# A fused attention, expert and feed-forward kernel: the first pair's q and k loaded in three pieces of columns in place of two

## The chip, the cores and the metric

The kernel runs on one core of a Trainium2 chip. The metric is the device time of one execution in microseconds (us): 481.08 us before the change, the median of three runs (480.73 to 481.11).

## The reference, cut to what matters

Three layers follow each other on a batch of 4 sequences of 448 rows. The first is causal attention with 12 heads of 64; the second routes rows to the best two of 4 experts, each an attention of its own; the third is a feed-forward block with a short convolution and a gate. Only the first touches the change:

```
batch, n_heads, seq, head_dim = (4, 12, 448, 64)
scores = scale * np.matmul(q, k.transpose(0, 1, 3, 2))
mask = np.triu(np.ones((seq, seq), dtype=bool), k=1)
scores = np.where(mask, -1000000000.0, scores)
scores = scores - np.max(scores, axis=-1, keepdims=True)
attn = np.exp(scores)
attn = attn / (np.sum(attn, axis=-1, keepdims=True) + 1e-09)
return np.matmul(attn, v).astype(np.float32)
```

The second and third layers (`_moe_ref`, `_moe2_ref`) take the result as `x`; their code is left out here, since nothing of theirs is edited.

## The kernel before

**Tiling.** Heads are handled in pairs, one head on partitions 0 to 63 and the other on 64 to 127. A sequence of 448 is cut into NQ = 4 blocks of CP = 112 rows. The mask is causal, so block i of the queries meets only the first 112 x (i+1) keys: the score of block 0 needs columns 0 to 111 of q and k, that of block 1 columns 0 to 223, that of block 2 columns 0 to 335, that of block 3 all of them.

**The first pair.** For batch 0 the pairs are "plain": `load_plain` brings q and k of both heads as one transfer of 448 KB into the tile `sk_A`. The very first pair differs: `load_left` (L563) brings columns 0 to 223 and `load_right` (L566) columns 224 to 447, 224 KB each. `pair_scores` multiplies q by k (L630) block by block, from block 0 up for this pair alone, and both heads one after the other in each block. `j.ready` lists the load that a block waits for: the left half for blocks 0 and 1, the right half for 2 and 3. Each score then goes through the row maximum on VectorE (L686), the exponential on ScalarE (L695), the division by the row sum (L347 or L349), the transposition on TensorE (L726) and the product with v (L797).

**What sets the order.** Every piece of work is a task, added with an engine, an estimated cost, the tasks that it needs and a `lag` (for a load, the estimated time from issue to landing; LAND is 2600 ns). The order in which the tasks are issued on all engines is written out by hand in the table ORDER, as numbers of tasks. `Program.run` walks this table and issues the tasks; on each engine they then run in that order, held only by semaphores. While it walks, `run` also keeps an estimated clock for each engine. It is used for one thing: where the estimate says that TensorE will sit idle for over 700 ns before its next task, `run` calls `fill` (`warm`, L1587), which puts so many multiplications of the 128x128 identity in front of that task:

```
if start - end[e] > 700:
    fill(int((start - end[e] - 200) / (260 if end[e] > COLD else 430)), end[e])
```

These fill multiplications write to a bank that nothing reads and wait for nothing but the engine. A task that `need`s a load starts, by this estimate, no earlier than the load's end plus its lag; that holds for a load that needs a load as well.

**The queue of SyncE (SP).** All loads at the start are issued by SP, in order: the left half, then two pairs of expert weights (`praw`, L950 and L951), the right half, the convolution weights, and the second pair's q and k (L558).

Of the kernel before, what the change touches and what calls it, by code (L numbers as in the profile page):

```python
# [35 lines left out]
    "xry9H9wXnQ!RRci4JAe@k$R*J=|Lut9mou_3)O={fDmXr8bEd-zaWFC1nM*L0+~aNqXtm-NDxYnMxpSiUy09%@39}S&xwB^#t=K$m&75|3~C<r"
    "0rd&RMo%DS5O%B!8^T^8chSR`bMyiF4n2WcM6IF@P^YLHlmJaZYtR<78x5e7=!fVB=p*zg8i`rM%wrC)N7yam5s`{HM=?sT(5zB%sj_s3ctb>z"
    "Mlm?dBIXvAM}aUbj1VKocrnwM6XFJD2XjZ<$KXMim~QkSnhNSgvq3bJ0Tl*~p(oJ8Xbt8Y@dxG<+gjRQI#xPgDg;fG1~6t!0@H!%EA7K{VfKi}"
    "m_tk!Gk{^CKqMTgwWy=0yXX~Bh>C&kF(@nzi^C3-Qb|LlY*J_G9Pur2h1f?LBTbMDrM6OU=>iET&4LC<o1`VuEP5WjgqD#&SQhppT7;b@nMpFx"
    "5NVaPP1+~rNi>Rr!lo>iPM5BgZkB2(dXkvrAtgwCMIMR_tHow19i%SOBTy#@#zXT4i$;njiU3NkC_^Ih=sXXvj|cEBu)UxhZvZq58sPcJ0rD;B"  # L40
    "taPumjS?W4DPKxIm0pzIm$vfSc{z}P5~FlcdMQ_>Aj%a9MZr;Su=iL{5wa*ren1{0Z;|ul_ryOytDsBL83{rrkSSyiSwJQf@pxjMk~am?^X5Q9"
    "lw&f2+)sH)nIKP-H$gj~N90cOQ}Q@vfxJXsCGUfF$a&Bi=o$GEL@VMHiHa0Ox*|)Fy9mNp@MkH@l)phBFcORh5Ajwh<Gd}(HigD#^A|u=u$IpT"
    "i@{3p9{HTy$&2x3cmn=4`6n642bIk8R(Njycght-LDrHzC4D8WB|ym^_EkHMAK>4Bbl_acJZ00qV^5VHQ1<P4yM_FT_kp*{JK&x2@D5yw8Eodq"
    "`2!{GC9_2fMaxC&MK`<`<gKFJA~*Oa1yKT}DyXeg3>8PEJLuG}_ALJy|1n?e;8MTYukCksup?Y_$m=Yjm5i6%@`g%~j(m~V(N2w(%#_F-z0|!T"
    "R*9(OwCJMfJ?$0P&f_^!Me`+Ehuxtov6Qqs9y@M|?u$HBfXXQr6|a=YO7avf^@P&K|He}k_wYyfkm4L)S8Of5pk7n|qDiP>@Fd?;94}trZ_qx`"
    "X81ty5+7AeEr!sLw0`PpiJ3~H$!QxUG3s{7LCI-JkK;4#nd6q)ft$p2QV&aTv~2OiVm57<dR~&Fb{0P^?!w`VZ%UpOKQEpJ-<AN58Qf8E(!s$C"
    "@k_XQu!bg}1@Z0pC9s9|vUsX^ruc2~9Cd}dQv8Pc1~*PUrd`r{aF9|&shjqYwg!&lH^KPQwc;2!L(78O!5@lOaWUEp#wg>3;}^#d+7x4svCcm&"
    "4$wCE>(pJU48KP`q7LGQaXZDIi!X}1z`fvS;G1F{9zsXb?~5V0ZSZICDDH%6!SC=ls4jdr4T0;Sb>eAsHeEp9#61V^;4X1raG!Asx|<%LYw3fu"
    "G1>$TkE7w%=@;~CI+&5c579R12XqcDPw&MK;6*qEPKW!4W8Cp4<8RuGW8SgkSaTp4X8J81M?a>Y;cjrZI0&AAr{d@EQ}~zo=lG9~-x({6cZ~n$"
    "e_(tCTX8NNfJ@;J_-)4l1H!yu#Oc?J1^gm@n|{j}1Fz$E@%xS}y`P?EP?>nfF$2lOF~9Kt$-j2|bikZchM1vY9D!L(wDT8S-f`lPF@(%E`niM4"  # L50
# [1601 lines left out]
```

## Time and profile before

| | |
|---|---|
| median of 3 runs | 481.08 us (480.73 to 481.11) |
| time of the profiled execution | 481.08 us |
| its span, first to last instruction | 479.3 us |
| around the span | 1.78 us |
| TensorE (PE) busy | 470.7 us, 98% of the span |
| VectorE (DVE), ScalarE (ACT), GpSimd (POOL) busy | 391.0, 347.4, 332.5 us |
| DMA | 93.26 MB, 195 GB/s on average |

PE is matrix multiplication, PEld the loading of its weights. A busy PE is not a useful PE: the fill multiplications count as busy too. One multiplication in f32 leaves two MATMUL records in the trace, so six fill multiplications show as x12. The work before microsecond 30 is a short sequence of few instructions, and the timeline there can be read one by one.

### The profile page before, as it was taken

To read this page: it belongs to the slowest core of one execution; us is meant where nothing else is said; L and a number is where in the kernel's file an instruction comes from. 1 tells how busy PE (TensorE), PEld (TensorE's weight loads), DVE (VectorE), ACT (ScalarE), POOL (GpSimd) and SP (SyncE) were. 2 spreads that over 40 slices of the span, in tenths; PEclk is the share of its full clock that TensorE was granted. 3 is DMA by queue.
4 is the path that set the end of the run, shared out by engine and by line. 5 is a ranking of instruction groups with operands and counts; after the bars stand their busy time and mean duration, and the time that the engine had idled before them with its cause. 6 is when DMAs were issued, how large, how long until landed. Compare 5 with 4: busy or idle time off the path is not lost.

```text
span 479.3 us, 9963 instructions
## 1 busy us (share of the span) xinstructions
PE 470.7 (98%) x3114; PEld 398.2 (83%) x3114; DVE 391.0 (82%) x1154; ACT 347.4 (72%) x966; POOL 332.5 (69%) x475
## 2 busy tenths in 40 slices
...
GB/s 216 197 227 93 218 171 236 277 271 177 218 217 180 283 251 181 196 157 203 251 212 133 175 166 205 275 77 247 198 226 214 276 291 128 234 216 77 40 77 96
DMA packets 45845, 93.26 MB, mean 195 GB/s; under 512 B 4832, under 2 KB 27232, under 8 KB 45792
## 3 DMA queue, kind: packets, MB, share of 16 engines
...
q8 instruction: 24, 0.39, 0.4%
q10 hardware_dynamic: 432, 0.34, 0.2%
...
## 4 chain that ended last, share of the span: by engine, by line
PE 84%; DVE 5%; POOL 4%; ACT 3%; issue 1%; DMA 1%; SPq 0%; POOLq 0%; ACTq 0%; DVEq 0%
PE bank L1471 22%; PE bank L797 11%; PE bank L991 11%; PE bank L726 10%; PE bank L673 9%; PE bank L1338 8%; PE bank L1042 6%; PE bank L918 3%; PE bank L630 2%; DVE P_A L686 2%; ACT P_A L695 2%; PE bank L1587 1%; DMA sk_M<-sk_M 1%; POOL P_M L349 1%; POOL P_A L349 1%
## 5 line engine op out<-in xcount | busy, mean ns | idle before, releaser
L695 ACT ACTIVATE P_A<-P_A,nm_A 112x224 f32<-112x224 f32 (+3 forms) x192 | 99.9, 525 | 10.3 <-DVE nm_A L686 9.7
L686 DVE CUSTOM_DVE_ANT_0 P_A<-bank,mask 112x448 f32<-112x448 f32 (+3 forms) x192 | 79.7, 441 | 10.0 <-PE bank L630 6.1
L356 POOL TENSOR_TENSOR sk_A<-nat,sk_A 64x448 fp32r<-64x448 f32 (+1 forms) x67 | 77.5, 1158 | 5.4 <-ACT sk_A L347 1.5
L991 PE MATMUL bank<-xT,wqk 128*128 128x448 f32 x288 | 66.9, 372 | 0.0
L726 PE MATMUL bank<-ident,P_A 112*112 112x112 f32 x480 | 60.6, 262 | 2.6 <-ACT PT_A L347 1.9
L726 PEld LDWEIGHTS bank<-ident,P_A 112*112 112x112 f32 x480 | 48.3, 133 | 9.4 <-ACT PT_A L347 2.7
L349 POOL TENSOR_SCALAR P_A<-P_A,r_A 112x112 f32<-112x112 f32 (+3 forms) x95 | 48.1, 519 | 10.0 <-DVE r_A L706 8.2
L991 PEld LDWEIGHTS bank<-xT,wqk 128*128 128x128 f32 x288 | 51.7, 188 | 3.9 <-DVE nm_A L686 0.2
L673 PE MATMUL bank<-sk_A 128*112 128x224 f32 (+3 forms) x288 | 52.0, 306 | 0.2 <-DVE nm_A L686 0.2
L1359 DVE SCALAR_TENSOR_TENSOR bank<-h,cw,bank 128x448 f32<-128x448 f32 x64 | 42.6, 685 | 9.2 <-ACT bank L1357 7.7
L797 PE MATMUL bank<-PT_A,v 112*64 112x448 f32 (+3 forms) x384 | 49.9, 404 | 0.0
L347 ACT ACTIVATE P_A<-P_A,r_A 112x224 f32<-112x224 f32 (+3 forms) x94 | 46.7, 527 | 2.8 <-DVE r_A L706 1.6
L1471 PE MATMUL bank<-up,ws 128*128 128x448 f32 x198 | 46.7, 367 | 0.0
L347 ACT ACTIVATE PT_A<-bank 112x336 f32<-112x336 f32 (+1 forms) x94 | 42.3, 476 | 4.7 <-PE bank L726 4.3
L797 PEld LDWEIGHTS bank<-PT_A,v 112*64 112x64 f32 x384 | 25.4, 136 | 23.1 <-issue 11.5
L1471 PE MATMUL bank<-us,ws 128*128 128x448 f32 x180 | 44.3, 366 | 0.0
L673 PEld LDWEIGHTS bank<-sk_A 128*112 128x112 f32 x288 | 40.4, 175 | 4.3 <-issue 0.4
L1042 PE MATMUL bank<-wvg,xT 128*112 128x260 f32 x288 | 43.5, 290 | 0.0
L1471 PEld LDWEIGHTS bank<-up,ws 128*128 128x128 f32 x198 | 37.2, 188 | 3.3
L1042 PEld LDWEIGHTS bank<-wvg,xT 128*112 128x112 f32 x288 | 36.8, 175 | 2.3 <-issue 1.1
L349 POOL TENSOR_SCALAR P_M<-P_M,r_M,g_w 112x336 f32<-112x336 f32 (+3 forms) x63 | 35.9, 584 | 3.1 <-ACT PT_A L347 1.4
L695 ACT ACTIVATION_READ_ACCUMULATOR P_A<-P_A,nm_A 112x1 f32 x192 | 37.6, 196 | 0.0
...
## 6 DMA issues: line engine op xcount, KB each, us to landing
nat<-in_qk_dram SPq DMA_DIRECT2D x72, 224.0 KB, 4.0
...
g<-g SPq DMA_DIRECT2D x32, 224.0 KB, 2.3
...
v<-in_v_dram SPq DMA_DIRECT2D x24, 224.0 KB, 4.8
out_dram<-osb_c SPq DMA_DIRECT2D x21, 224.0 KB, 2.0
```

The lines of the kernel that those rows point to most:

```text
L347: nc.scalar.activation(dst, src, AF.Copy, scale=scale)
L349: nc.gpsimd.tensor_scalar(dst, src, scale, 1.0 if scale2 is None else scale2, ALU.mult, ALU.mult)
L356: (nc.gpsimd if e == "POOL" else nc.vector).tensor_tensor(dst, a, b, op)
L673: nc.tensor.matmul(sp[:CP], t[:, j.o[h], m * CP : (m + 1) * CP], t[:, j.o[h] + k, :w], start=(k == 2), stop=(k == 1),)
L686: nc.vector.tensor_tensor_reduce(rows(i), st["s", i][:CP, :w], mask[:, S - w :], -SCALE, 3.0e38, ALU.add, ALU.min, st["nm"][:, i : i + 1],)
L695: nc.scalar.activation(rows(i), rows(i), AF.Exp, bias=st["nm"][:, i : i + 1], scale=-1.0, accum_out=st["sm"][:, i, 0:1],)
L726: nc.tensor.transpose(pt[:CP, o : o + CP], rows(i)[:, kt * CP : (kt + 1) * CP], ident[:CP, :CP])
L797: nc.tensor.matmul(st["ov"][h * D : (h + 1) * D, kt * CP : S], j.v[:, kt, h, :], j.PT[h][:, col_base[kt] : col_base[kt] + S - kt * CP], st ...
L991: nc.tensor.matmul(st["ps"][:, :S], proj["wqk"][:, a, cc, w, p * P : (p + 1) * P], xT[b, cc][:, b2, :], start=(cc == 0 and (a, b2) == PASS ...
L1042: nc.tensor.matmul(st[i][:CP, :VW], xT[b, cc][:, a, i * CP : (i + 1) * CP], proj["wvg"][:, b2, cc, :], start=(cc == 0 and (a, b2) == PASSE ...
L1359: nc.vector.scalar_tensor_tensor(y, h, w, y, ALU.mult, ALU.add)
L1471: nc.tensor.matmul(ps(pb)[:, :S], wset[s][:, a, m, c2 * P : (c2 + 1) * P], unit(operands[q, c2, name][0])[:, b2], start=(c2 == 0 and (a, b ...
```

## The change

The first pair's q and k come in three transfers. `load_left` now brings columns 0 to 111 (112 KB), and `load_next` brings columns 112 to 223 (112 KB) and columns 224 to 447 (224 KB). Block 0 waits for the first piece, block 1 for the second, blocks 2 and 3 for the third. Each load task names the one before it as needed. The estimated costs and lags of the three tasks are new, and the table ORDER has one step more, the second piece, between the scores of block 0 and block 1; its other steps are the same tasks in the same sequence, with numbers one higher.

```diff
-    "c-jrt$4}b{gD_xMa0ORz1y^tdS8&DMxPpH!xPwh*B_LS|NLB(ep9Ew+2}oAL<Xwr9l_*&$kU3E103-(>IRKdhkUd~B2TBeBascwK1Y}nFzUQxa"
...
+    "c-jru*)JRlqX6((&CaaM%B;-Ftjx;nW@UD>o8jC9?M={g6SOx$&rQ&C6SOxm`rX9Ro1nc((Fe<UK>L990X+}s_h9rqSo%=(0sU@rzrW&_9~vTr"
...
         def load_left():
             alloc_head(j, 0)
             j.qk = f(j.sk[0][:, 0:2, :])
-            nc.sync.dma_start(j.qk[:, :, : S // 2], qk[j.b, j.p, :, :, : S // 2])
-
-        def load_right():
-            nc.sync.dma_start(j.qk[:, :, S // 2 :], qk[j.b, j.p, :, :, S // 2 :])
+            nc.sync.dma_start(j.qk[:, :, :CP], qk[j.b, j.p, :, :, :CP])
+
+        def load_next(k):
+            cs = slice(CP, 2 * CP) if k == 1 else slice(2 * CP, S)
+            return lambda: nc.sync.dma_start(j.qk[:, :, cs], qk[j.b, j.p, :, :, cs])
...
         if j is order[0]:
-            t = add("SP", 700 + dma(224), load_left, take=[j.skb[0]], lag=LAND + 150)
-            j.ready = [t, add("SP", dma(224), load_right, [t], lag=LAND + 300)]
+            t = add("SP", 1200, load_left, take=[j.skb[0]], lag=LAND)
+            t2 = add("SP", 600, load_next(1), [t], lag=LAND)
+            t3 = add("SP", dma(224), load_next(2), [t2], lag=LAND + 300)
+            j.ready = [t, t2, t3, t3]
         elif j.plain:
             t = add("SP", dma(448), load_plain, take=[j.skb[0]], lag=LAND)
-            j.ready = [t, t]
+            j.ready = [t] * NQ
...
             t = add(
-                "PE", 2 * (CP * (i + 1) / 1.2 + 95), score(i), ([j.ready[i * 2 // NQ]] if j.kind == "A" else j.ready[0]) + first,
+                "PE", 2 * (CP * (i + 1) / 1.2 + 95), score(i), ([j.ready[i]] if j.kind == "A" else j.ready[0]) + first,
                 take=take, free=[j.skb[0]], mode=2,
             )
```

What stands first on TensorE's queue before (L1587 are fill multiplications, L630 with 112x112 is block 0, with 112x224 block 1, with 112x336 block 2; `bank` is a PSUM bank, `sk_A` holds q and k, and the brackets name the semaphores waited for, DMAHW those of transfers):

```order
L1587 MATMUL bank_65<-ident 128x128 [waits Pool_49]
L1587 MATMUL bank_65<-ident 128x128 x5
L630 MATMUL bank_61<-sk_A_0_145 112x112 [waits DMAHW0_49]
L630 MATMUL bank_62<-sk_A_0_145 112x112
L630 MATMUL bank_65<-sk_A_0_145 112x224
L630 MATMUL bank_67<-sk_A_0_145 112x224
L1587 MATMUL bank_63<-ident 128x128 x9
L630 MATMUL bank_68<-sk_A_0_145 112x336 [waits DMAHW5_49]
L630 MATMUL bank_62<-sk_A_0_145 112x336 [waits DVE_49]
```

The same place now (lines are three higher, so L1590 is the fill and L633 the scores):

```order
L1590 MATMUL bank_65<-ident 128x128 [waits Pool_49]
L1590 MATMUL bank_65<-ident 128x128 x4
L633 MATMUL bank_61<-sk_A_0_145 112x112 [waits DMAHW0_49]
L633 MATMUL bank_62<-sk_A_0_145 112x112
L1590 MATMUL bank_68<-ident 128x128 x9
L633 MATMUL bank_65<-sk_A_0_145 112x224 [waits DMAHW1_49]
L633 MATMUL bank_67<-sk_A_0_145 112x224
L1590 MATMUL bank_63<-ident 128x128 x11
L633 MATMUL bank_68<-sk_A_0_145 112x336 [waits DMAHW6_49]
L633 MATMUL bank_62<-sk_A_0_145 112x336 [waits DVE_49]
```

One fill multiplication fewer stands before block 0, nine stand between blocks 0 and 1 where none stood, and eleven in place of nine stand between blocks 1 and 2.

What stands first on SP's queue before, `praw` being expert weights and `cwraw` the convolution's:

```order
L563 DMA sk_A_0_145<-in_qk_dram 128x2x224
L950 DMA praw_169<-in_w_qk_dram 128x512
L951 DMA praw_169<-in_w_vg_dram 128x260
L950 DMA praw_177<-in_w_qk_dram 128x512
L951 DMA praw_177<-in_w_vg_dram 128x260
L566 DMA sk_A_0_145<-in_qk_dram 128x2x224
L1227 DMA cwraw<-in_conv_w_dram 128x24
L558 DMA sk_A_1_209<-in_qk_dram 128x896
```

And now:

```order
L563 DMA sk_A_0_145<-in_qk_dram 128x2x112
L567 DMA sk_A_0_145<-in_qk_dram 128x2x112
L953 DMA praw_178<-in_w_qk_dram 128x512
L954 DMA praw_178<-in_w_vg_dram 128x260
L953 DMA praw_186<-in_w_qk_dram 128x512
L954 DMA praw_186<-in_w_vg_dram 128x260
L567 DMA sk_A_0_145<-in_qk_dram 128x2x224
L1230 DMA cwraw<-in_conv_w_dram 128x24
L558 DMA sk_A_1_220<-in_qk_dram 128x896 [waits DMAHW0_49]
```

The second piece stands directly behind the first and waits for nothing; everything behind it stands one place later, and the ninth transfer waits for the first one's semaphore.

## Rows read from the trace of the kernel before

**Rows 1.** The page: the span, and busy us of each engine.

```profile
span 479.3 us, 9963 instructions
...
PE 470.7 (98%) x3114; PEld 398.2 (83%) x3114; DVE 391.0 (82%) x1154; ACT 347.4 (72%) x966; POOL 332.5 (69%) x475
```

**Rows 2.** The chain of waits, 0 to 9 us and behind: start us, us, what.

```profile
1.36 2.93 PE bank L1587 x12
...
4.29 1.40 PE bank L630 x8
5.68 2.77 PE bank L1587 x18
8.45 0.74 PE bank L630 x3
...
9.28 0.51 DVE P_A L686
9.79 0.42 DVE P_A L686
```

**Rows 3.** Timeline, 0 to 8 us: start us, us, engine, line, operation, idle before.

```profile
0.73 0.69 SPq L563 DMA_DIRECT2D sk_A<-in_qk_dram  x1
1.36 2.93 PE L1587 MATMUL bank<-ident 128*128 128x128 f32 x12 [1.36 <-POOL ident masks.py:199]
1.47 0.58 SPq L950 DMA_DIRECT2D praw<-in_w_qk_dram  x1
3.52 0.58 SPq L566 DMA_DIRECT2D sk_A<-in_qk_dram  x1
4.21 1.47 PE L630 MATMUL bank<-sk_A 64*112 64x112 f32 x8
4.78 0.43 SPq L558 DMA_DIRECT2D sk_A<-in_qk_dram  x1
5.73 0.39 DVE L686 CUSTOM_DVE_ANT_0 P_A<-bank,mask 112x224 f32<-112x224 f32 x1 [0.34 <-PE bank L630]
7.16 0.42 DVE L356 TENSOR_TENSOR wvg<-praw,wvg 128x260 fp32r<-128x260 f32 x1
7.61 0.33 SPq L950 DMA_DIRECT2D praw<-in_w_qk_dram  x1
```

**Rows 4.** Timeline, 8 to 32 us.

```profile
8.38 5.16 PE L630 MATMUL bank<-sk_A 64*112 64x336 f32 x24
9.28 0.51 DVE L686 CUSTOM_DVE_ANT_0 P_A<-bank,mask 112x336 f32<-112x336 f32 x1 [1.70 <-PE bank L630]
16.34 1.57 PE L630 MATMUL bank<-sk_A 64*112 64x448 f32 x8
24.74 0.83 PE L630 MATMUL bank<-sk_A 64*112 64x224 f32 x8
```

**Rows 5.** Transfers one by one (left half, right half, two later ones): KB, us to landing.

```profile
sk_A<-in_qk_dram SPq DMA_DIRECT2D x1, 224.0 KB, 3.1
...
sk_A<-in_qk_dram SPq DMA_DIRECT2D x1, 224.0 KB, 3.9
...
sk_A<-in_qk_dram SPq DMA_DIRECT2D x1, 448.0 KB, 4.3
...
praw<-in_w_qk_dram SPq DMA_DIRECT2D x1, 256.0 KB, 3.2
...
sk_A<-in_qk_dram SPq DMA_DIRECT2D x1, 448.0 KB, 5.3
```

**Rows 6.** Timeline of PE alone, narrow windows between 2 and 8 us.

```profile
2.58 1.70 PE L1587 MATMUL bank<-ident 128*128 128x128 f32 x7
...
4.21 0.72 PE L630 MATMUL bank<-sk_A 64*112 64x112 f32 x4
...
4.72 0.96 PE L630 MATMUL bank<-sk_A 64*112 64x224 f32 x4
...
5.61 0.79 PE L1587 MATMUL bank<-ident 128*128 128x128 f32 x2
...
6.41 0.81 PE L1587 MATMUL bank<-ident 128*128 128x128 f32 x4
...
7.06 0.72 PE L1587 MATMUL bank<-ident 128*128 128x128 f32 x5
```

**Rows 7.** Line 1587 in windows: us, PE busy, PEld busy, clock, DMA share, GB/s.

```profile
3.40:3.70 0.30, 0.30 (x4) 0.30 (x3) 1.00 0.94 348
...
7.00:7.30 0.30, 0.30 (x5) 0.30 (x5) 1.00 1.08 320
```

**Rows 8.** Line 1587 before 4.25 us and from 6.4 us: durations ns min/median/max.

```profile
L1587 PE MATMUL bank<-ident x12: 421/421/582, 1.4 to 3.9; 128*128 128x128 f32 x12
...
L1587 PE MATMUL bank<-ident x17: 274/275/421, 6.0 to 8.2; 128*128 128x128 f32 x17
```

**Rows 9.** Waits of SP's queue, 0 to 14 us: us in total, times, longest.

```profile
SPq L950 <- DVE wvg L356: 1.7, 1, 1.7
```

More of the change, by code (lines that the diff above doesn't have):

```diff
@@ L36 @@
[L36 to L50, printed above, removed]
@@ new lines @@
+    ";O2rrK}$ibz**2%&<VrBT`&qf02_vl!g^u-Fai8a!TW;Kg6jehOb^(C@51k305}sag`XD~0Xf(-Yz_v8<>6=W0mK#j7OsJ>V{Qw^5GHsOo`EmJ"
+    ")?x2qPQVCs44Q);z^4(%@I}N50*4?YfCxBZ7j_K0fStguU@U|Hu?Kqt#lt8t7Hk4BgqTCP;X!x@ybs<FAAyg-JK=hy3mHKEf_Z>>gxN&wAodVv"
+    "hz}?PsvX&hR3LN+3&M>EAX*UJh&DtovL6WtU{MrQ4AG1DiijgykY5njh#YbXIgA7$;YbY%kE9@fBRnH~z<k6!C;S1QgzsZs5=N2p$VKEw<Y%M+"
+    "H4UGKdoVss0&|NvK#ifVP{$}BdK$fg+&~^9FOc_0DT;|QqMRr{Du!xBJwiP|ouV#KIP@lZ5q*p~#q1JJ2`uy#l3Q|%;+H5&bS3+QdjgI)fhMC@"
+    "&;V2(2}kqMGPDLAM9-nm3ESv>G>~|N#sO~7eW(!>1u%eO0oX_@G6a}JO{2z8M)Y^WPxJ+*qok{3vShJD0GKX`q8;cKbT@jiWDwnpJ|vu>Ptfh?"
@@ new lines @@
+    "VKg5JCz6RBh24dHg|7%QWE23x;4y3r88ckMB94{_h&?5*3Co0a!XR;yI8C&cxJ!a1OT<`77BEcQA+8b^P>ZNll$r>~@G+lIa?BjjL6ibUi5tW{"
+    ";t?@VWRtaI0ePilu4J=hr^H0I5EaA#v4uET7$B=LCQLiIo7hWy2<QZ$xdiS=;dtS6VT_zBY$MXR9BzO+$c=HYF};8scK|R980LmZQ4)Z3S#ns?"
+    "Nsba7<gX>4ORh^m<PL5ZcMKpUXUM(e0rG7LoP0~flgZ?J45$!Zh%0O*Js?ezc1d~C2f{nR3gCu#Nko#UBqm8nl9H%}Vy=R#<Gut~xU+y!@)-$B"
+    "8X~_WPm|_In}8j_ucRK*Q_>W9iL^@EAngP8Nk@RMfM=vj0J~6FC@<6&nhTwU{z4>A%Ud9?k^cbz01-eOaFn}2p5pG3_sDFXfVTjk08Km=Py|!}"
+    "4@p;~9&Uy^&z17-NZ?`|4_>^;UFZ6FKghRaEy+X*6b}}66vvAHux?n%yeRJ)patfN7s)%;ed{kJ$K)ex-s&WM=6>XEaF4kcT#AicYy>)ZS>AAQ"
@@ new lines @@
+    "SMfsOQsG+RR^dJO1!=eNpwI~fQ?SJ-ik8wrAyUW`j*Ub4W^Ly^<2~jnY$D2c>zx&7L)emqC)}Q5cJWj(fHzu<v*inewk}Ghc)nO;8=xE(@{8rg"
+    "7lqe_AE<u=dbncSFNKT6CY#4*E_N1o*&f^O3qeHzN{k{bk{7KPtBdnw6Xl%T$@|XL7WMPSdB~z1&s^jxx~AMw{-P==A>a%zP?RlN;%!quQ|EcH"
+    "qE#Ngh*gB7;;2KEjbaCdP1R7hi!+qH;^X3r;(pr~>N6XF+KrvT_E1iW$<+3uM@0ha80D%sN9iegTGWfB6x|m;D|%iu1q77DZ1dRDqE?#_C&R5`"
+    "=YdA5lp4o%;TC~T>dT_pqWPlbqSusl%6idT%3JId<&1hm?Z+ZZuqA%#BkC$Ji`xWJN;Zq4z&2_Y*be+yw1Le~U(hG$FKiEOKdH0y*YqvkMNyQx"
+    "&D)|JP}I0X$|+?8JBHma`ciaV)CKGXJ_X(vnQ=%Ojt0UavD?7UzzOU*#fjVJZBu->J}MU5Pwm06X#$#*wu5~J+{fNvzhb{&wKP91N;A<$sFT!b"
@@ new lines @@
+    "Dh12NZqcr3cQgdO4L3^Np&iqN*gS0jH;j{GwOBLuZ?-AhpL7Uq-nM94wQbt4bO#MUC)3Vom)LtO0Efg;aV*?x+$`=T?m6z0?Hzrc{+|AK-beah"
+    "Ko{1BjbVSmVsU%6V>*&?P0!Nq=u5a2+#U_U7zb|Q4sb`dcG?gvPiHYG^fNk+L1ujA{eyRB1KZJd7F|I%(vN|B2EqOio41|Y)N~o6lXhhj(fesV"
+    "G!27d=h($|g*|9b*vA=Lj3dSl;|RBnJ7Gi_ImQ%YkFh{qq%JTP87qu&+6--pHc!jZER0oZ#@=rK)xJWz#|iN=ya^A)`xt<72jiS^$wQUvL01ey"
+    "=?xEDdIr1#zNv80<Ma-CCp|;=(NA$_I6R($*VylX7Q4sZ!suqSF_!SF_+2~@ga8phG|(Vpn6ZyP#h>E|<qmug<CdYu!%N|KCf<*~!}rnq>Fjc9"
+    "sjzgI9>cfdAK;B3Y3U=pw%k<y7%wOflsiFwPz;m>Jperd9pbg6#!_bK+luuHHt4uKUyiK6ReZ<uL9B`mJb-{8#L8tL9Dzf4Um+sU2nvF$)K?lS"
@@ new lines @@
+    "Z7IDjzbofg=p9Cf)8Th~s@SXeQt`E-qcl@Kh#$f`%G=93%cbSx_!)e6X<z9ao?iaY5p!f6osPlMk<zi!CxYt=Bp=7mmG+ji`2xO%Z{$xn2FhQS"
+    "&pMu$FFUk^nNk<QN4Tp1@OvEtj$y}dpoP+<(zVj9(lN*11aBOGia4QPFf4d3*e%^FJu3aHbb)`&&-430tB!rgrsI?2#_`i(B3zf=m(G@-m1hW`"
+    "GGrOPj9hWWmsMygw)oUCLD^6_nJ?u#`F{QczJt(32v#^M08W&XSvCYp@E`Cq{6+o>f1&(s`3_%RrY$p<xyp_lfwFj6ds(Jzt$d?=w|uWWQDLcQ"
+    "sc5U%672E2D+ViuDtao$KsnGfXh$#)x)$6C9`XD51N;#_LU_wR;{yf9g1lgoKgFj@5P~uOx6&mRQ?knHF6%2BEE_2sFPkizFPkp=>i7iO0}-9y"
+    "9QRDD;0TllorA7G;}y9IAZu3eTCgl&3b4X6fk>i|EQ8iTWC33w7nlV?7C`tDq?eqsOswgObCyG(7VHV`Sh9c8yHvJTwpF%UhG$V&2W0_4Q~(Aa"
@@ new lines @@
+    "mz|g8%PbPN<f`mv8AZqvChIfx?e$&tz4dSwfY~Qp5bm<}Sp)S0LY)xBBrs`A4pYRGG5wM)5E3jEI#@;_U-+FhE_4aw!kln}rDIx{PG*q#gz$U)"
+    "X#F7z3*HpQn2SOL8^>O$e_!9q{9LbQF<BkLPT`brTj*!SSgkAyxP#fvY?0*Zr|Z8}v<QZTD?*>}chL`AM(7dwMB|d2WM0z89Axeb=j#{i59^PF"
+    "--RR0C-z6I$E*jeK~|q+m^IE6u@!6@o5R+!jqDuL#r{-3AUP493FGW6dz#rUX%ln_ehL$!uk{N|Y9*_3i8;=iVXZM;mHx_X<xPF7=&pWB@>cSP"
+    ";GyV|=&@)>;$wG8RwbK~uac)Cd8MYZt#XdFCz)VHE8p0^)o(F(nFq`xW}XQW!9|CXZHcjxUpX#X5amQ$q9YMr#1;`8JEA=i&B1i^RZ&C&5!m4p"
+    "_ld{EU6ljkA@P)GQPf+xBJzu0D051Iql4YWJ`tUZ`t4VuVf&a}F4Bkwt41rM;tBDE<X!@({4Ti_wTMTm+QpsXmzB>dpH|LP&Q~HUmnv5(zcB~d"
@@ new lines @@
+    "Tb0|DCK0xBT0E;Hh=<vuY?OFj{7(5+3>I&Tm)NW99d^z>UNy<4ikV`eSSp@oPusQPA51OB#OdG+a9%5ql}7P<@w)gxd@9Z>yEsZmQnIdmul%Sy"
+    "7b8{IVwNhviE*x#XvZ(rzf~Vp&awB{8|))?o(<;QDc{;x?T2Cq=T;1oY}yYi^OZYxoNC|xlRd85Qsq>a>>D<cb7bF9-B(dLAZZV0h?C)rao`dx"
+    "2cUXT{iynJb&j*jIa1*yQ!29R&d%ZpIa1D^YC(mR;-!nKh3c*9*PL0-GAD1RO1C%%oE^@Iimy85oN*?rW~z>>k2u$y#p<2v71g=wN_D1`sq)nt"
+    ")nZjt<xu%l&#IqSzpQ3UTWaR3_)?|%9T-@@QVp*DW)G?1)wdkAy1hmwHL0%bxO%PBEOki((u>Ntv_*=pe^pJcAFpXqwMn~GgQ~0QF6oe}v*xyX"
+    "t!k^PuO_NCsh#TGs)MTIs_V)&m7<<dt*f7}G1c!?_oz;*&a1AfdZqW3peke)zKT;nP%~8HuIGaJ;9QLi{8L4)VpX-OAE>F-ed=-bRLz2VQ~kE)"
@@ new lines @@
+    "tQuIO0k76<)*xyY)y(P@@KfoK^svSR7FMsQwbjOIVU@f}TScyUF8x#YMfX*gQ#-)}>TR{Odb`G4<*GWV;n#ew`Bg2h4^+jfvQ^j8dnrgJ*Z9Dj"
+    ";2m&_rdKni=F|{sUP>=@v(nenA+<(h)U<2%)ko@njlAZf=6lUP_z3LM_%$c$Gj*pXs?pSZSKq2b^*?k!b<5IKDOmqr`cZmc15^)d#x!p=6PiDj"
+    "u4;evzSLaftU=1~vOrC=hAIPT5SlO2hgE~JVOd^^*RVBY4N|=%i&c-x_?k)Cv}{f`r;*DbTAX@SwjtY*?a8#VU#qloliVQ>$Yb&j`K)G5Gaw(5"
+    "cgcI?R6R@Y();yU{jO$TbF7i;QCfobQu-B)(jVwS2Bu6PqpA@Gnl=Hx1Ru%rGO%2uzmZ+ae#$m955XQMU*8Gt1rLC^+KhZmo|C_pFUx1;X4!?_"
+    "C1a`uYNR|MYttL`QT>trM4#7C<ybjWE|g2<ahXd?F?8v#^u78CeZT%zk2MT~$H0BsG3|s_q+OS9$q(eGa)nl>J(NG!XJrH0c9~z>0?vVF!603W"
@@ new lines @@
+    "R<6_Nm<EACW(XQA2DjmrVa~8@&>5oIcI~!&NZ+YFmpgSn9YVKmxX@5_EZq|}-N|$coZmHfnj!74vJZy;bI#}&z;k-OZb`qQ$Lc;BJ{x3Cjnm|u"
+    ")*5wN`fYtom(>yVPh?i@y!O3zS^H7zbH)wV;9GEyu2Z+Jy)axEIt+b=enZTeb@n=+I)8UQcT#I*wXE89XO}Z$Xw!8X`gPZGqyne-VmQ#AYOl42"
+    "+A}S`_D-8~&N|;XZ{^EQbuHVdRhSfh#g<}6@!9#s34}xyw}uhjsLr97)J^HG6$s^m?oI)!Mbu(z*$RPT)%lm<z4MdPRJ*8i*0$CrYK2C*F<3iO"
+    "yH<NpdsKT~yIDJ5OIGYDq>8MfUGZ4)RPjjhOfg~@Ge8tML*98(`@MF%wypMU?OiRfj!;Ld<J6(*u*x;vhOWD|w|200sP<Sfu9#6wDDsLk1wgr@"
+    "yL3Xh^NR7>T<vMyMV+utTj#1X*2(H9N|sWm6e%sr>pHD*NwKQ%)y3;Fbqb|R=~Kp)9m-B+d)*J`|G1zojEm&DuLBv8Mv9T<zHw)ieM+;@WsDiI"
@@ new lines @@
+    "#(t&W*j?9GH(2-0b>o7#;qITVg}RZtrMk7c@w%<L-MY!Tsk(zYg8SYL@W4Gsb-Siv^SSA%=MUEhm(J5-eCJ}jah@3?-z{}(+$OifePGI&JB;1N"
+    "KI5Iq?@qcY9;Ro(xMW;2ZW%v%rpyA5(lcn>HSQZnjAO=}@z^wPMwpL`W{<<;^Ta$^&xmK#GvS%`w0ZKzF3%HBtNYS;YFahVdk#E@o)gcxhhmPK"
+    "T1*|LZd0FW(Db{q!+quXZu)NgX?*Kh^?dMvO(@fb8EXcZZ#_US+RHQx%mgph``W$aCYWd@mPuq%m^3Df$!Qugb-I~ezIWV|^iG;)ObezZ)0#<U"
+    "{_G8!f@YnW;c}aKE{RL!GPo?}xVgh@bG-@mxMkh}x5hi{erp~z@0j<^EA9>Vj(gOdbML!by}x?Dnm0_JT(8`h<}c<O^8@ee2BX*MJ#?EbKr7tp"
+    "vUHg<=6iG2(q_R~$<{7QkEPE%U=COYEJK#ZUY3<_MOvs9mIY@CdE*wDb<6^=OjxEZ^On5(n>*}!>OJ<Jc+b37-aD_Z(cGxEIvRbAvBqrUQp2al"
@@ new lines @@
+    "m4=Omod&PV6Mp7>ZviwQ8i)=5;rdV4e#5wT!aL=i_nNFu>v~9Nky^fm4;%Ix--nhh>z0p}1Ixd-PAzAae8XRji{5VyZH--xhn5xZruUQgN#jk!"
+    "eFLBo-iT|YH2xk5H1#!ITW&4126h9#;Y(wywYA}aHE2y(r45>fj)u;LZtI|R*!r|_q><SuXjC@73kjQgtUV2h@NF0#8E7yyj9VwHp|GRD-;iv$"
+    "Y`ke~^>_F?{XPEHaJ)(0G~6)YANG$nPBcz8jyB{PUNwLtElu-{H~xG7f4N5efWVA(-ulk^wsEx)9>4`YH0muW*N^bOy8g}e@2(e-mk~l_HbMz7"
+    "1KK8<pY8t`;`^ok&!L&7&%R@yK9KXj@(TjWfW`MX+|l$beBwLvUHR^OE}zdg*fi3l@td2XzO3&{=$Y>_)b8tSY73kEkHTZ&)yQ0A+z0TFH%&Bw"
+    "qR8k$6F!;`Ek@o)ZbO~E3ExE67zhP=eF#6%4-7vI&xRd-zdz~!&G+9fN7F*nQWG`0*0kC5sp+`se_emN2BW7<Q@(lMMblN&Kbn3vevBMOK)#V^"
@@ new lines @@
+    "JlYcdJ@ML4i6Fv@z7^l5@00H@mnfo%$fMfml7B7?_u<0#(SxWdG9EQY^AT5cGTIUCj$VaW5ohFcFc@J)#nEVB#lPX-@$dT=qKo0<=u#Bx%LWep"
+    "z0th?+dtz)@v(e-pUkKCT}Ir2;~+A28eI<1!Z(qN=t_7y?2pny?9hH>I(ia}M$Up)!Mh+J^mi8`^dRsvvKH6~aKh|ZJoY}^5?hOI2lfL;fs?>_"
+    "pf&O=I3B!;@<Y;)CNvQQH+>FI1?PjNkR#*|B|{yt?pSZ^x7dS-BJwCQ9>d2dv90K2Y$hfO{|qd|KtXtLGqxD}BSsAU2z-mThPng7m^?Nd!v-nA"
+    "o<M(KI4~Aagb%}C!`j%3gfQL_lE>jqv?fl|eGC-eiTY!vm?t(7m=3%NbcV!9T+?psAf^jj!i&L`U{8n@<OeOm$B~HyGOmr|<D0>O&~$<l=f*!J"
+    "KLuSuUvMB2kGI5+V;%AC_-bM}G#a{#%Yyn~Z~V77FcA&TB}U?F@zdB=+#KJHAH<L1f5m^qmC0Nv8*C4b$JbJm@vW3DX-U3M?4~+W-KoQ5XRtST"
```

59 lines of the change are left out of this document (7 added, 52 removed).

## The prediction

> **What bounds the kernel now.** I read the page first. PE is busy 98% of the span [rows 1], which by itself says little, because fill multiplications count as busy. So I went to the chain of waits and followed it from its beginning. It starts with PE: twelve fill records at 1.36 us, the scores of blocks 0 and 1, eighteen fill records at 5.68, then the score of block 2 at 8.45, and only from there into DVE's row maxima at 9.28 [rows 2]. The reader should see that no transfer stands in this stretch of the chain. PE's own queue sets it, and over half of what that queue does there is fill.
>
> The timeline says the same from the other side. DVE sits idle 1.70 us before the row maximum of block 2, released by PE [rows 4]. The transfers, taken one by one, confirm it: the left half is issued at 0.73 and lands 3.1 us later, at 3.83, while block 0 starts at 4.21; the right half is issued at 3.52 and lands 3.9 us later, at 7.42, while block 2 starts at 8.38 [rows 3 to 5]. Both halves lie ready, 0.38 and 0.96 us, until the fill in front of their score has run out. So the place to count is PE's queue from 1.36 us to block 2.
>
> **The rate of the fill.** Before block 0, seven records take 1.70 us and one lasts 421 ns, so they start (1.70 - 0.42) / 6 = 0.213 us apart. Near the end of the second fill five records take 0.72 us and one lasts 274 ns: (0.72 - 0.27) / 4 = 0.111 us apart [rows 6, 8]. The step lies between the records at 6.41 and those at 7.06; I put it at 6.6 us. The column of the granted clock reads 1.00, the 2.4 GHz level, in both stretches [rows 7], so it does not show this step and I count with the records. PE had no gap worth naming from 1.36 us on, and it has none in the changed queue either, so I leave the step at 6.6.
>
> **The change, part by part, along PE's queue.**
> - Before block 0 stand five fill multiplications in place of six, two records fewer: 2 x 0.213 = 0.43 us. Block 0 starts at 4.21 - 0.43 = 3.78. The first piece must have landed by then. Its rows give no direct price. It carries half of the left half's bytes from the same issue, so it lands no later than 3.83 unless small runs are slow; if they double its cost per byte it is still 3.83. From below, half of the 3.1 us would be 2.3. I take it as landed; the other end costs 0.1 us.
> - Block 0 holds PE from 4.21 to 4.72 before [rows 6], 0.51 us; now from 3.78 to 4.29.
> - Then come nine multiplications, eighteen records, where none stood. At 0.213 up to 6.6 us that is 2.31 / 0.213 = 10.8 records; the other 7.2 at 0.111 take 0.80. They end at 7.40. Before, the last slow fill record and the following score were 0.13 us apart (3.87 + 0.21 against 4.21), so block 1 starts at 7.53, against 4.72.
> - The second piece is issued where the first expert weight was, at 1.47. That one, 256 KB, took 3.2 us [rows 3, 5]; for 112 KB in the same place I take the same, 4.67, and even the 5.3 us of a 448 KB transfer would give 6.8. It is covered by the nine fill multiplications until 7.53.
> - Block 1 held PE from 4.72 to 5.61 at the slow rate, 0.89 us [rows 6]. The same two shapes together take 1.47 us there and 0.83 us later on, when PE runs at the fast rate [rows 3, 4]; so 0.89 x 0.83 / 1.47 = 0.50, until 8.03.
> - Then eleven multiplications in place of nine: 22 x 0.111 = 2.44 us, and 0.03 for the handover: block 2 starts at 10.50 against 8.38. **That is 2.1 us later.**
> - SP's queue is one issue longer, 0.58 us by the row of the same kind. The right piece is issued at 4.10 and with 3.9 us lands at 8.0, covered until 10.50. The second pair's 448 KB go from 4.78 to 5.36 and land 4.3 us later at 9.7 [rows 3, 5], before block 3 is done. Its new semaphore is that of the first piece, long landed.
>
> **What else is late, and what hides it.** DVE and ACT work through blocks 0 and 1 and two expert weights before block 2. DVE begins block 1 at 5.73 and ends the second weight at 7.58 [rows 3], 1.85 us. Now block 1 reaches DVE about 0.57 us after 7.53 (1.01 us before, at the fast rate 1.01 x 0.83 / 1.47), so it is done with the weights at 9.95. Block 2's row maximum, 9.28 + 2.1 = 11.4, still finds DVE idle. Hence the whole delay passes into the chain, and no more than it. SP's next weight load waits for DVE's `wvg` [rows 3, 9] and slips from 7.61 to about 10.0, 2.4 us. Behind it stands the third pair's load: issued at 9.39, 5.3 us to landing, so there at 14.69, and used at 16.34 [rows 4, 5], a cushion of 1.65 us. It loses 0.3 of that. Nothing from here on starts from the program's beginning: loads wait for engines, engines for the chain. So I carry the 2.1 us to the end undiminished.
>
> The sum is made against the profiled execution, whose 481.08 us (479.3 of span and 1.78 around it) equal the median of the three runs: 481.08 + 2.1 = 483.2 us.
>
> **A rule that could shift the size.** The rows show the step at about 6.6 us, after PE had run fill, then scores, then fill. The Trainium skill ("TensorE: Matmul & The Clock Gate", Part 1) says that activity of the array releases its throttle, in a rhythm that does not restart with the kernel, so that the moment varies between runs. By that rule the changed queue may get the step at another time.
>
> **Rivals.**
> 1. *The fast rate comes earlier*, because from 4.7 to 5.6 us fill now stands where the scores of block 1 stood. For it speaks only that what PE does before the step is no longer the same. Against it, that PE was already busy without a gap and still got the step only at 6.6. If it came at 4.8: 0.51 / 0.213 = 2.4 slow records, 15.6 x 0.111 = 1.73, block 1 from 6.66 to 7.16, block 2 at 9.63. That is 1.25 us late: 482.3 us.
> 2. *The fast rate comes later*, after the eighteen records of the new fill: 4.29 + 18 x 0.213 = 8.12, block 1 from 8.25 to 8.75, block 2 at 11.2: 2.8 us late, 483.9 us.
> 3. *The delay is swallowed* (not slower). The place would be a later stretch in which every engine waits for transfers that started regardless of the first scores; from 2.1 us of such slack on, nothing is left and the time is 481.1, with half of it 482.0. If the early scores of block 0 also carried something, 0.43 us could come back: 480.65. For it speaks only that the first pair is a small part of the span. Against it: the chain begins at the very fill that grows, and SP's loads wait for engines from 7.61 on, so they slip along.
> 4. *The extra fill is not in the way*, since it only runs while PE would wait for the pieces. That is what fill is for, and it would hold if the second piece truly came around 7 us and the third around 10. The load estimate in the code says so, because the second load needs the first and so its estimated start lies behind the first one's landing. But SP's queue shows no such wait, and the left and right halves landed 3.1 and 3.9 us after their issue. If pieces did land so late, the time would be about the forecast's all the same, with PE idle in place of fill.
>
> **How the numbers follow.** Forecast, with rival 4's same time: 0.66. Rival 1: 0.12. Rival 2: 0.10. Rival 3: 0.12, of which I give 0.09 to a time within 0.2% and 0.03 to something faster than that. A measurement of this kernel can tell about 0.2%, 0.96 us, from no change, so slower means above 482.04: the forecast and rivals 1 and 2, 0.88, less 0.03 for the lower edge of rival 1, which comes to the same: 0.85. Same 0.12, faster 0.03. The forecast's own spread, with the step between 6.0 and 7.2 us and 0.3 us of chance in the long rest, is 482.6 to 483.7. The range reaches to rivals 1 and 2 and a part of rival 3: 481.6 to 484.1.
>
> **What would show it.** In the changed profile: ten fill records before block 0, which starts near 3.8; eighteen between blocks 0 and 1, with block 1 near 7.5; twenty-two before block 2, near 10.5; DVE's first row maximum near 4.7 and that of block 2 near 11.4 behind an idle time released by PE; all three pieces landed before PE reaches them; and the same later steps 2.1 us later than before, at microsecond 30 and at the end. I am wrong if block 2 starts within half a microsecond of 8.4, or if the steps at 30 us are late by 2 us and those at the end are not.

## The result, and the profile after

The changed kernel takes 483.99 us (median of five runs, 482.77 to 485.18) against 481.08 for the kernel before: 1.0062 times, 95% interval 1.0046 to 1.0078, or 2.9 us slower. The forecast was 483.2. The profiled execution is the slowest of the five, 485.18 us, so its trace holds more than the median's loss.

The chain of waits of the changed kernel from 1 us to block 2 (start us, us, what):

```profile
1.36 2.50 PE bank L1590 x10
3.86 0.65 PE bank L633 x4
4.51 2.52 PE bank L1590 x18
7.03 0.56 PE bank L633 x4
7.60 2.65 PE bank L1590 x22
10.25 0.80 PE bank L633 x4
...
11.08 0.51 DVE P_A L689
```

It is the chain of [rows 2] with ten, eighteen and twenty-two fill records in place of twelve, none and eighteen. No transfer stands in it. The timeline beside it, same columns as [rows 3]:

```profile
0.74 0.69 SPq L563 DMA_DIRECT2D sk_A<-in_qk_dram  x1
1.48 0.59 SPq L567 DMA_DIRECT2D sk_A<-in_qk_dram  x1
3.79 0.72 PE L633 MATMUL bank<-sk_A 64*112 64x112 f32 x4
4.18 0.55 SPq L567 DMA_DIRECT2D sk_A<-in_qk_dram  x1
4.68 0.28 DVE L689 CUSTOM_DVE_ANT_0 P_A<-bank,mask 112x112 f32<-112x112 f32 x1 [3.65 <-PE bank L633]
6.96 0.64 PE L633 MATMUL bank<-sk_A 64*112 64x224 f32 x4
7.65 0.39 DVE L689 CUSTOM_DVE_ANT_0 P_A<-bank,mask 112x224 f32<-112x224 f32 x1 [2.68 <-PE bank L633]
10.18 4.16 PE L633 MATMUL bank<-sk_A 64*112 64x336 f32 x20
11.08 0.51 DVE L689 CUSTOM_DVE_ANT_0 P_A<-bank,mask 112x336 f32<-112x336 f32 x1 [1.58 <-PE bank L633]
```

Block 0 starts 0.42 us earlier than before, block 1 2.24 us later, block 2 1.80 us later (10.18 against 8.38). The transfers of the first two pieces and of the third, by their landing times:

```profile
sk_A<-in_qk_dram SPq DMA_DIRECT2D x1, 112.0 KB, 2.6
...
sk_A<-in_qk_dram SPq DMA_DIRECT2D x2, 112.0 KB, 2.8
...
sk_A<-in_qk_dram SPq DMA_DIRECT2D x1, 224.0 KB, 3.8
```

The first piece lands at 0.74 + 2.6 = 3.3, the second near 1.48 + 3.0 = 4.5 (2.8 is the median of the two), the third at 4.18 + 3.8 = 8.0. Each lies ready, for 0.5, 2.5 and 2.2 us, until PE has done its fill. The fast rate begins near 5.1 us here, not at 6.6, as windows of 0.3 us show (x is the number of fill records that overlap each):

```profile
4.60:4.90 0.30, 0.30 (x2) 0.30 (x3) 1.00 1.04 296
4.90:5.20 0.30, 0.30 (x4) 0.30 (x4) 1.00 0.73 245
5.20:5.50 0.30, 0.30 (x5) 0.30 (x4) 1.00 0.77 284
```

From block 2 on, the instructions are 1.8 us late, within 0.1 us, up to 126 us. Two things come later in this execution. First, the granted clock is at 0.50, the 1.2 GHz level, for 3.4 us; before that PE was thinly used (2.79 of 4 us). The third row is the same place in the kernel before, as thinly used, behind which the clock stays at 1.00:

```profile
124.00:128.00 4.00, 2.79 (x21) 1.92 (x21) 3.13 (x7) 3.17 (x10) 3.79 (x5) 1.00 0.62 192
128.00:131.40 3.40, 3.40 (x17) 1.43 (x13) 2.38 (x10) 2.58 (x6) 2.54 (x3) 0.50 0.63 176
...
122.00:126.00 4.00, 2.81 (x24) 2.00 (x23) 3.14 (x7) 3.18 (x10) 3.84 (x6) 1.00 0.66 197
```

PE's transpositions go from 1.8 to 3.2 us late over this stretch. Second, a load of q and k (`nat`, 448 KB in two transfers) lands late near 275 us. The issue, the step of POOL that waits for it, and the transposition of the expert pair's P that comes some 21 us behind the issue, first in the kernel before and then in the changed one:

```profile
266.06 1.59 SPq L542 DMA_DIRECT2D nat<-in_qk_dram  x2
...
271.58 0.95 POOL L349 TENSOR_SCALAR sk_A<-nat 128x896 fp32r<-128x896 f32 x1 [0.93 <-DMA nat<-in_qk_dram]
...
287.50 0.99 PE L726 MATMUL bank<-ident,P_M 112*112 112x112 f32 x7
```

```profile
268.72 1.58 SPq L542 DMA_DIRECT2D nat<-in_qk_dram  x2
...
275.74 0.94 POOL L349 TENSOR_SCALAR sk_A<-nat 128x896 fp32r<-128x896 f32 x1 [2.40 <-DMA nat<-in_qk_dram]
...
291.70 1.01 PE L729 MATMUL bank<-ident,P_M 112*112 112x112 f32 x7 [0.75 <-POOL P_M L349]
```

From issue to that transposition it takes 21.44 us before and 22.98 now: POOL waits 1.5 us more, and PE then waits for POOL. At the end of this trace the steps are 4.2 us late: 1.8 from the start, 1.4 behind the clock stretch, 1.5 behind the load, 0.3 near 155 us, and 0.9 given back near 165 us. The clock stretch and this load are not in the prediction. The experiments ask which of them belongs to the change.

### The profile page after: what moved, and what is told of

Its sections match the earlier page's. It is cut to its first block, busy times and chain, and to the rows that moved or that the text cites. A ratio compares the mean times of both kernels' runs of the same rounds, so it can differ in the third digit from the quotient of the medians.

```text
span 483.4 us, 10005 instructions
## 1 busy us (share of the span) xinstructions
PE 474.0 (98%) x3134; PEld 401.0 (83%) x3134; DVE 390.3 (81%) x1154; ACT 347.7 (72%) x966; POOL 333.1 (69%) x475
## 4 chain that ended last, share of the span: by engine, by line
PE 84%; POOL 7%; ACT 3%; DVE 3%; issue 1%; DMA 1%; SPq 0%; POOLq 0%; ACTq 0%; DVEq 0%
PE bank L1474 21%; PE bank L994 11%; PE bank L800 11%; PE bank L729 10%; PE bank L676 8%; PE bank L1341 8%; PE bank L1045 7%; PE bank L633 2%; PE bank L921 2%; ACT P_A L698 2%; PE bank L1590 2%; POOL P_A L349 1%; DMA nat<-in_qk_dram 1%; POOL P_M L349 1%; POOL wom L356 1%
```

## The experiments

Ratios are against the kernel before, run on the same chip in the same session. Runs e1 to e4 share a session, e5 to e8 the next one, e9 and e10 a third, e11 a fourth, each on another chip; across sessions ratios are compared, not times. `FILLS` gives the fill of PE's first tasks in place of the estimate; e4 and e10 are the two kernels unaltered.

**1. Fill alone, and pieces alone.** The first kernel takes the kernel before and the second the changed one; each takes over only half of the change.

```diff
+FILLS = (5, 9, 11)        # e1, in the kernel before
+FILLS = (6, 0, 9)         # e2, in the changed kernel
...
-                if start - end[e] > 700:
+                if turn < len(FILLS):
+                    fill(FILLS[turn], end[e])
+                elif start - end[e] > 700:
```

> The kernel before with its two halves and its queue of transfers, and only the fill multiplications of the changed kernel: 5, 9 and 11 in place of 6, 0 and 9. Theory (the fill in PE's queue is the whole delay at the start): block 2 starts near 10.2 us as in the changed kernel, 1.8 us later than before, DVE's later row maxima are 1.8 us late up to 120 us, and the time is 1.8 us or more above the kernel before: 482.5 to 485. Rival (the third transfer, its small runs and the longer SP queue make the delay): block 2 waits for no transfer, and the time is that of before plus at most the fill that no load covers, under 481.6.

> The changed kernel with its three pieces, but with the fill of the kernel before: 6, 0 and 9. Theory (fill is the cause, pieces are harmless): block 2 starts near 8.4 us, the time is 480.7 to 481.5, as before. Rival (pieces or the shifted semaphores cost): block 2 waits for the third piece, or later steps are late, and the time is above 482.

> The changed kernel, unaltered, once more beside the three others. Of its 2.9 us, 1.8 are there at 10 us; in the profiled execution 1.4 came with a stretch of half clock near 129 us, and 1.2 with a transfer of q and k that landed late near 275 us, of which some was given back near 165 us. If the part over 1.8 us is chance, this execution has other late places than the first one and the time again spreads over 2 us between 482.8 and 485.2. If it belongs to the program, the same places are late by the same amounts.

Fill alone: 484.19 us, 1.0072 times (1.0055 to 1.0088). The changed kernel again: 484.31, 1.0074 (1.0058 to 1.0091). Pieces alone: 481.47, 1.0016 (1.0001 to 1.0031), just above no change. So the two halves with the new fill are as slow as the change itself, and the three pieces with the old fill are nearly as fast as before. In the pieces-alone kernel block 2 starts at 8.43 against 8.38, and there PE does wait for the third piece, its fill being over:

```profile
8.43 3.42 PE L637 MATMUL bank<-sk_A 64*112 64x336 f32 x17 [0.97 <-DMA sk_A<-in_qk_dram]
```

That trace also has a stretch at the 1.2 GHz level from 14.5 to 18 us; from 60 us on its steps are 0.7 to 0.9 us late. Of its 12 runs, 6 have a mean clock of 0.996 or less, against 6 of 23 of the kernel before in the same session. So the fill is shown to be the cause of the delay at the start. Of the pieces no more than 0.1 us at block 2 is seen in a trace; whether PE's wait for the third piece costs the rest of the 1.0016, by way of the clock, was not tested.

The three traces with this fill do not have the same delay at the start. Block 2 begins at 10.18, 10.74 and 11.31 us, and the fast rate of the fill near 5.1, 6.3 and 7.4. The last, of the fill-alone kernel, in windows of 0.3 us:

```profile
7.00:7.30 0.30, 0.30 (x4) 0.30 (x3) 1.00 0.90 306
7.30:7.60 0.30, 0.30 (x4) 0.30 (x4) 1.00 0.75 294
7.60:7.90 0.30, 0.30 (x6) 0.30 (x4) 1.00 0.65 263
```

The later the step, the more records run at 0.213 us. The Trainium skill ("TensorE: Matmul & The Clock Gate", Part 1) says that this moment varies between runs of one kernel; the two traces of the changed kernel agree, with 1.2 us between them. The stretch of half clock at 128 us is in one of the three only, although PE is as thinly used there in the second trace of the changed kernel (2.79 of 4 us from 124.5); and a mean clock of 0.996 or less stands in 3 of 17 runs with this fill, no more often than in the kernel before. So it does not belong to the change. The late load is in all three.

**2. Why the late load comes with the fill.** In the window in which the load is under way, the changed kernel's transfers include one more than the kernel before's. Columns: queue, kind, packets, MB, share.

```profile
q1 hardware_dynamic: 580, 1.32, 97.7%
q14 instruction: 1, 0.01, 0.7%
```

```profile
q1 hardware_dynamic: 715, 1.61, 99.1%
q8 instruction: 1, 0.02, 1.1%
q14 instruction: 1, 0.01, 0.4%
```

The first is the kernel before, 266 to 271.6 us, the second the changed one, 268.7 to 275.7. Queue q8 brings instructions in packets of 16 KB; the page of the profile counts 24 of them before and 25 after, and PE is the engine that got more instructions, so I read it as PE's. One such packet takes 0.9 to 1.9 us in these traces. Ten fill multiplications more are twenty weight loads and twenty MATMULs, so each later packet comes that many PE instructions earlier in the program. Before, the sixteenth starts at 273.3, when the load has landed; now at 272.2, when it has not. The other transfers do not explain the difference: the eight others issued from 5.2 us ahead of the load to 3.5 us behind its first issue stand within 0.1 us of the same places in both traces. That gave a test: change the number of instructions without the time, and the time without the number.

```diff
+TINY = {4: 1, 5: 3, 6: 3, 7: 3}   # e5 in the kernel before, e9 in the changed one
...
+                if turn in TINY:
+                    fill(TINY[turn], end[e], 4)   # the last number is w
...
+                nc.tensor.matmul(t[:w, :w], ident[:, :w], ident[:, :w], start=True, stop=True)
...
+FILLS = (128, 230, 282)           # e6 in the changed kernel: columns of the 5 + 5 + 5 fill multiplications
...
+                    fill(5, end[e], FILLS[turn])
...
+                    nc.tensor.matmul(t[:, :w], ident[:CP, :], mask[:, :w], start=True, stop=True)
```

> The kernel before, loads and fill untouched, with ten multiplications of 4x4 more on PE, placed in the gaps in which PE waits for DVE between the second pair's scores (1, 3, 3, 3). As many instructions more as the changed kernel has, and hardly any time at the start. Theory (the part of the delay that appears at 275 to 290 us comes from where PE's own instruction fetch of 16 KB falls: with 40 instructions more, the 16th fetch slides ahead of the end of a q and k load that POOL waits for): steps are late by under 0.4 us up to 270 us, the 16th fetch lies 2 to 4 us earlier in the program, that load lands 1 to 1.5 us later than before and steps from 290 us on are 1 to 1.5 us later than at 260; time 481.4 to 482.3. Rival (that loss belongs to the size of the delay at the start, which shifts the loads against something fixed in time): no loss at 275 to 290 us, time as before, 480.4 to 481.2.

> The changed kernel with about the same time of fill in as few instructions as the kernel before had: 5 multiplications of 128 columns, 5 of 230 and 5 of 282 (the mask as moving operand) in place of 5, 9 and 11 of 128. Theory (two parts: fill time at the start, fetch place later): block 2 is 1.8 to 2.9 us late as in the changed kernel, but steps at 290 us are no later against before than at 260, and the time is 481.8 to 482.9, 1.3 us or more below the changed kernel. Rival (all of it is start delay): the loss at 275 to 290 us is there again and the time is 483.8 to 484.5.

> The changed kernel with the ten small multiplications of the earlier experiment on top: PE now has 80 instructions more than the kernel before and does strictly more work. Theory (the place of the 16 KB instruction fetch decides the late loss): the 16th fetch slides a further 4 us forward, to before the q and k load issued near 268.7 us moves its data, that load lands in under 5.2 us, steps at 290 us are no more than 0.4 us later against before than at 260, and the time falls to 482.6 to 483.5. Rival (the late loss follows the delay at the start, or any extra instruction adds): the loss at 275 to 290 us stays at 1.2 to 1.5 us and the time is 484 to 484.6.

> The kernel before, unaltered, for a second trace of it. If the 0.9 us that nearly every other trace gives back near 165 us was a chance slowness of the one profiled execution, this trace is 0.6 to 0.9 us ahead of that one from 170 us on, apart from what the start of the fast rate and stretches of half clock add. If it belongs to the kernel, it stays where it was.

The wide fill has the delay at the start (block 2 at 10.22) and takes 482.91 us, 1.0052 (1.0031 to 1.0073), at the very top of the 481.8 to 482.9 expected. That is 0.5 to 1.1 us less than the narrow fill by the ratios (1.0062 to 1.0074), but the intervals overlap. The changed kernel with eighty instructions more takes 483.35, 1.0053 (1.0041 to 1.0066): by the ratios 0.4 to 1.0 us less than without the last forty, though it does more, again with intervals that overlap. The kernel before with forty more takes 481.02, 1.0014 (0.9995 to 1.0033), under the range forecast and not clear of no change: a miss. Its trace starts 0.5 us ahead of the first trace of before at block 2 (7.85), with an earlier fast rate, which hides part of the loss in that trace; it does not explain the median of twelve runs. So the times agree with the packet and do not prove it. The traces, one of each run, put the time from the load's issue to the transposition beside the place of the packet:

| kernel (in order of the packet's place) | block 2 starts | load issued | q8 packet starts, us behind the issue | transposition, us behind the issue |
|---|---|---|---|---|
| before, again (e10) | 8.66 | 265.46 | 7.5 | 21.39 |
| before | 8.38 | 266.06 | 7.3 | 21.44 |
| pieces alone (e2) | 8.43 | 266.93 | 7.3 | 22.06 |
| wide fill (e6) | 10.22 | 267.54 | 5.4 | 21.71 |
| changed | 10.18 | 268.72 | 3.4 | 22.98 |
| changed again (e4) | 10.74 | 268.38 | 3.2 | 22.67 |
| fill alone (e1) | 11.31 | 268.34 | 3.2 | 22.91 |
| before, more instructions (e5) | 7.85 | 264.88 | 3.0 | 22.51 |
| changed, more instructions (e9) | 11.47 | 268.24 | 0.7 | 22.03 |

Rows of four of them: the kernel before again, the kernel before with more instructions, the wide fill, and the changed kernel with more instructions:

```profile
265.46 1.58 SPq L542 DMA_DIRECT2D nat<-in_qk_dram  x2
...
286.85 0.99 PE L726 MATMUL bank<-ident,P_M 112*112 112x112 f32 x7
```

```profile
264.88 1.59 SPq L546 DMA_DIRECT2D nat<-in_qk_dram  x2
...
287.39 1.01 PE L730 MATMUL bank<-ident,P_M 112*112 112x112 f32 x7 [0.80 <-POOL P_M L353]
```

```profile
10.22 1.57 PE L637 MATMUL bank<-sk_A 64*112 64x336 f32 x8
...
267.54 1.58 SPq L546 DMA_DIRECT2D nat<-in_qk_dram  x2
...
289.25 1.00 PE L733 MATMUL bank<-ident,P_M 112*112 112x112 f32 x7
```

```profile
268.24 2.01 SPq L546 DMA_DIRECT2D nat<-in_qk_dram  x2
...
290.27 1.01 PE L733 MATMUL bank<-ident,P_M 112*112 112x112 f32 x7 [0.73 <-POOL P_M L353]
```

With the packet 3.0 to 3.4 us behind the issue that time is 1.1 to 1.6 us longer, whatever the delay at the start: the kernel with the earliest block 2 has it, and the wide fill, as late as the changed kernel, has not. The four kernels of the next experiment fit too: the packet starts 6.5 to 7.5 us behind the issue and that time is 21.42 to 21.71. A further forty instructions take off about half, leaving 0.64 over 21.39, where I expected at most 0.4; the load then lands 5.9 us behind its issue, where I expected under 5.2. That the place of this packet decides the late loss is shown by the three edits that move it, and all thirteen traces fit but one: the pieces-alone kernel's 0.7 us without such a packet is unexplained. How the packet holds the load up is not shown.

The kernel before, run again, takes 480.36 us, 0.9993 (0.9981 to 1.0004). Its second trace is 0.9 us faster than the first between 160 and 170 us, and the others but that of the pieces alone are faster there by 0.5 to 0.9. So the first trace of before had a chance loss there.

**3. Less waiting before block 2.** Since PE's queue sets the start, the load of the right half can go in front of the expert weights and the fill behind it can go.

In the kernel before, the right half's step in ORDER is moved directly behind the left half's, in all four.

```diff
+FILLS = (6, 0, 0, 0, 0, ...)   # e3
+FILLS = (6, 0, 0, 0, 9, ...)   # e7; e8 also moves the weights' steps on DVE and ACT behind block 2
+FILLS = ((6, 128), (0, 128), (0, 128), (0, 128), (4, 282), (1, 128), (1, 128), (1, 128), (2, 128), ...)   # e11
```

> The kernel before with the right half issued directly behind the left one, ahead of the expert weights, and 6 fill multiplications before block 0 but none before the next twenty tasks of PE. If PE's queue in front of block 2 sets the start, block 2 begins near 5.7 us, DVE goes on without a pause up to the second pair, whose load lands near 9.2, and the time falls by 1 to 1.7 us: 479.4 to 480.1. Rival (fill is needed for PE's rate, or the expert weights now come too late): the gain is under 0.5 us or negative, 480.6 or more.

> Right half issued behind the left one, 6 fill multiplications before block 0, none before blocks 1 to 3, and the 9 others before the second pair's scores, where PE otherwise waits for their load from 6.7 to 9.3 us. As many instructions as before. If what took the gain of the halves-first kernel was PE's half clock from 14.4 us after too idle a stretch, this keeps the clock up and gains 0.5 to 1 us: 479.6 to 480.1. Rival (the expert weights, which now land later, took the gain): as before, 480.4 to 481.

> The same with the expert weights' two steps on DVE behind block 2's row maxima, and the two on ACT behind its first exponential, so that neither engine waits for the weights' landing with scores ready. If landing of the weights is what the halves-first order loses, ACT's exponential of block 3 starts near 9.5 us against 10.15 there and 10.96 before, and the time is 479.1 to 479.8. Rival (POOL, which gets the weights later, takes it back at the first division): no better than the kernel with fill alone.

> Right half behind the left one, and fifteen fill multiplications as in the kernel before, but spread over the gaps of PE: 6 before block 0, none before blocks 1 to 3, 4 of 282 columns while PE waits for the second pair, 1 before each of its next three scores and 2 before the first transposition. Over half of the runs of the halves-first kernels without that spread had a stretch of half clock (mean clock 0.996 or less), and their runs without one were 478.7 to 480.8. If PE's thin use between 9 and 14 us is what lets the clock fall, at most 2 in 10 runs have such a stretch and the median is 479.0 to 480.0, 0.6 us or more under the kernel before. Rival (the fall is not to be had from these gaps, or the fill now delays the scores): as many such runs and a median of 480.3 or more.

In order: 480.78 us, 1.0012 (0.9994 to 1.003); 480.81, 0.9993 (0.9975 to 1.0012); 480.28, 0.9995 (0.9977 to 1.0014); 480.30, 0.9989 (0.9975 to 1.0003). By the ratios each beats the changed kernel by 2.4 us or more, none the kernel before beyond its interval, and all four miss the times expected of them. In the first, block 2 starts about 3 us earlier, but ACT and DVE then wait over 1 us for the weights, and the second pair's load lands only at 9.3. In the third the weights no longer hold ACT up, and the exponential of block 3 starts at 9.43, as expected, but the time does not follow. The first kernel's trace shows the clock at 0.50 after a thin stretch of PE (3.42 of 4.4 us busy); in the pieces-alone kernel PE was busy 3.97 of 4.5 us before the fall:

```profile
10.00:14.40 4.40, 3.42 (x22) 2.33 (x20) 3.79 (x21) 4.40 (x16) 3.29 (x8) 1.00 0.88 281
14.40:21.20 6.80, 6.48 (x27) 3.95 (x26) 4.49 (x16) 4.23 (x16) 2.85 (x6) 0.50 0.73 229
```

A mean clock of 0.996 or less stands in 9 of 12 runs of the first, 5 of 12 of the second, 3 of 12 of the third and 2 of 12 of the last; in the kernel before, in the same sessions, in 6 of 23, 9 of 30 and 6 of 17. (The first three make 17 of 36, just under the half that the expectation of e11 names.) The count of the spread fill is as low as expected, but with 3 of 12 without the spread, that the spread lowers it is not shown. The median did not reach 480.0, and the gain stays below what these runs can tell.

## Why the prediction was right

- **PE's queue bounds the start: right.** No transfer is in the chain in front of block 2, before or after, and the fill alone reproduces the whole loss (1.0072 against 1.0074). The mechanism held; the size came out low, and 483.99 stands only 0.1 us inside the range, whose upper end came from rival 2, a later step that this trace does not have. The changed kernel run again, 484.31 and 1.0074, lies outside. That the range held was partly luck.
- **Block 0, 3.78 forecast, 3.79 measured.** The first piece landed in 2.6 us, between the ends that I had given.
- **Block 1, 7.53 forecast, 6.96 measured; block 2, 10.50 and 10.18.** Two terms failed, in opposite directions. The step, put at 6.6, came near 5.1 in this trace, the direction of rival 1; by the forecast's own sum that gives block 2 at 9.78. And the sum is 0.40 us short on the handovers between scores and fill: 0.15 into the second fill (from 4.44, not 4.29), 0.07 in block 1 (0.57, not 0.50), 0.18 in the third fill and its handover (2.65 in place of 2.47). The traces with other steps show the same: with 6.3 the sum gives 10.35, measured 10.74, and with 7.4 it gives 10.88, measured 11.31. In this trace the two errors nearly cancelled, which was luck.
- **2.1 us at the start.** The three traces with the fill of the kernel before and its two loads (before, e10, e5) start block 2 at 7.85, 8.38 and 8.66; the four traces with the changed fill at 10.18, 10.74, 11.31 and 11.47. The means lie 2.6 us apart, 0.5 more than forecast, about what the handovers explain.
- **The third piece and the second pair are covered: right.** The third piece landed at 8.0, and the second pair, issued at 5.41 and 4.5 us under way, at 9.9, before PE came to them.
- **Rival 4 is refuted.** It held that the fill stands only where PE would wait. The second and third piece landed 2 us and more before their scores.
- **"I carry the 2.1 us to the end undiminished": right in that nothing was swallowed, wrong in that nothing was added.** The forecast counted the time of the added multiplications, and left out that they are also forty more instructions. In the traces the place of a 16 KB instruction packet makes 1.1 to 1.6 us of difference. In the times it is smaller and not clear of noise: 0.5 to 1.1 us between narrow and wide fill by the ratios, and 0.7 us (-0.2 to 1.6) for forty instructions in the kernel before. So two terms of the sum were too low, the handovers at the start and this one, at nothing; how the missing 0.8 us divide between them, the times do not settle.
